# Moving stores between two DMA queues, and a prefetch by one unit, in a routed-attention and ELU-MLP kernel

## The chip, the cores and the metric

The kernel runs on one core of a Trainium2 chip. The metric is the device time of one execution in microseconds, lower is better. Five engines work beside each other, each on its own list of instructions in order: TensorE (PE, with its weight loads PEld), VectorE (DVE), ScalarE (ACT), GpSimd (POOL) and SyncE (SP). In this kernel SP does nothing but ask for DMAs, and what it asks for waits in the order in which it was written.

## The reference

Attention over q, k, v of shape (4, 8, 768, 64) in float32, in which a query sees only the keys of its own cluster, and then a two-layer MLP over the 3072 rows of 512 that come out:

```
mask = q_assign[:, :, :, None] == k_assign[:, :, None, :]
scores = np.where(mask, scale * np.matmul(q, k.transpose(0, 1, 3, 2)), -1000000000.0)
attn = softmax(scores)
x = np.matmul(attn, v)                  # -> (3072, 512)
h = x @ w_in                            # w_in (512, 2048)
g = np.where(h > 0.0, h, np.exp(np.minimum(h, 0.0)) - 1.0)
out = g @ w_out                         # w_out (2048, 512)
```

## The kernel before, in words

**Attention** comes first, in 32 slots of one batch, half a sequence and two heads each. Beside its last slots GpSimd prepares sums of x and of w_in for what follows, and VectorE still turns the last pieces of w_out, which arrive as 64-bit words, into float32 (`begin`, `join`, L306 to L350: L316 and L324, then ACT's L326, then L336, L340, L346). A piece's buffer comes free after L340, and then SP asks for the next (L296).

**The MLP** then takes six groups of 512 rows (k_ = 0 to 5). Each group has a first product (x times w_in, with the ELU) and a second (g times w_out). Both are done with a block scheme that needs seven block products in place of eight, at the price of sums and differences of blocks of weights and of activations.

*First product.* Four units u = 0 to 3 (`unit`, L752). A unit has seven block products of eight matmuls (L726), in this order: a11, s1, s2, a12, s3, s4, a22. a11, a12, s1 and a22 are parts of w_in itself; s2, s3 and s4 are sums of them, and stand in three places of the tile `spare` (`w_tmp`), which every unit uses again. In group 0 GpSimd computes them for the next unit (`w_step`, L705, L707, L709, one each for s2, s3, s4) and a DMA stores each in DRAM (`w_far`, L710). In groups 1 to 5 a DMA loads them back (L702). `w_step(k_, u + 1, n)` is called inside unit u: n = 0 and 1 in its body, n = 2 in `rest_of`, which runs at the start of the next unit (`flush_all`). Behind the products ACT copies banks (L766, L770, L775, L783) and takes the exponentials (L736), GpSimd clamps them (L737), VectorE adds banks (L776, L785) and finishes the ELU (L740, L802). The block s3 waits for ACT's copy L775, the block s4 for VectorE's L776.

*Second product.* Group 0 does it plainly (`second_product_plain`). Groups 1 to 5 do it once more by the block scheme (`second_product`, L1035, small products of four matmuls, L901). Its right sides are sums of parts of w_out, the tables. They are made once, in group 1, by `table_steps` (L850): seven parts of w_out, s3, s4, s2, a11, a12, s1, a22 in this order, four steps of VectorE each (L859, L862, L866, L869), with a store to DRAM after each (`far_w`; seven stores for s3, s4 and s2, three for the other four, called DIRECT). Results stand alternately in `sums_w` (`s_all`) and `p_out`. A unit of group 1 calls `fill_table`, two steps, four times, the last of them in `rest_of`.

*Streaming.* The second product reads the tables through ten places in SBUF (`slots_w`: four in `words_w`, five in `sums_w`, one in `p_out`). `fetch` (L896) loads the next in the order of use; after each use one more is fetched. The first ten are fetched after unit 2 of group 1 (L1174).

So on SP's list of group 1 stand, in the order of the code, the loads of `w_far`, the stores of the tables and the first ten fetches, and each of them waits for what stands ahead of it.

Of the kernel before, what the change touches and what calls it, by code (L numbers as in the profile page):

```python
# [61 lines left out]
def main_path(ctx, tc, c, q, k, v, centroids, moe_w_in, moe_w_out, out):  # L62


    nc = tc.nc
# [82 lines left out]
    slots_w = [words_w[:, ts(n, 512)] for n in range(4)]  # L148
# [525 lines left out]
    def x_parts(k_):  # L674
        a, b_ = slice(GS * k_, GS * k_ + QS), slice(GS * k_ + QS, GS * (k_ + 1))
        return X[:, :2, a], X[:, :2, b_], X[:, 2:, a], X[:, 2:, b_]
# [13 lines left out]
    def w_parts(u):  # L690
        low, high = slice(QS * u, QS * u + QS), slice(DF // 2 + QS * u, DF // 2 + QS * u + QS)
        return w_in[:, :2, low], w_in[:, 2:, low], w_in[:, :2, high], w_in[:, 2:, high]

    w_far = [[far.tile([P, 512], F32, name=f"w_far{u}{n}") for n in range(3)] for u in range(4)]

    def w_step(k_, u, n):

        a11, a12, s1, a22 = w_parts(u)
        s2, s3, s4 = (w_tmp[:, m] for m in range(3))
        flat = spare[:, 0, ts(n, 512)]  # L700
        if k_ > 0:
            nc.sync.dma_start(flat, w_far[u][n])  # L702
            return
        if n == 0:
            nc.gpsimd.tensor_tensor(s2, s1, a11, op=Alu.subtract)  # L705
        elif n == 1:
            nc.gpsimd.tensor_tensor(s3, a22, s2, op=Alu.subtract)  # L707
        else:
            nc.gpsimd.tensor_tensor(s4, a12, s2, op=Alu.subtract)  # L709
        nc.sync.dma_start(w_far[u][n], flat)  # L710

    def blanks(s):

        for bank in sets[s][1:3]:
            nc.tensor.matmul(
                bank,
                lhsT=blank,
                rhs=blank[:, 0:1].to_broadcast([P, 512]),
                start=True,
                stop=True,  # L720
            )

    def block_product(bank, left, right, first):
        for f in range(2):
            for ch in range(2):
                nc.tensor.matmul(  # L726
                    bank[:, ts(f, QS)],
                    lhsT=left[:, ch, ts(f, P)],
                    rhs=right[:, ch],
                    start=first and f == 0 and ch == 0,  # L730
                    stop=ch == 1,
                    skip_group_check=True,
                )

    def elu_exp(to, bank):
        nc.scalar.activation(to, bank.rearrange("p (f n) -> p f n", f=2), Act.Exp)  # L736
        nc.gpsimd.tensor_scalar(to, to, 1.0, 0.0, op0=Alu.min, op1=Alu.max)  # L737

    def elu(to, bank):
        nc.vector.scalar_tensor_tensor(  # L740
            to, to, -1.0, bank.rearrange("p (f n) -> p f n", f=2), op0=Alu.add, op1=Alu.max
        )
# [3 lines left out]
    def flush_all():  # L746
        flush()
        for other in behind:
            other()
        behind.clear()  # L750

    def unit(k_, u, after_second=None, fill=None):  # L752

        fill = fill or (lambda: None)
        x11, t3, x21, x22 = x_parts(k_)
        t1, t2, t4 = x_s
        a11, a12, s1, a22 = w_parts(u)
        s2, s3, s4 = (w_tmp[:, m] for m in range(3))
        b1, b2, b3, b4 = sets[(k_ + u) % 2]
        m5, u3 = stage[:, 0], stage[:, 1]  # L760
        low, high = slice(2 * u, 2 * u + 2), slice(FC // 2 + 2 * u, FC // 2 + 2 * u + 2)
        c11, c12 = g[:, low, :QS], g[:, low, QS:]
        c21, c22 = g[:, high, :QS], g[:, high, QS:]

        block_product(b1, a11, x11, True)
        nc.scalar.copy(b2, b1)  # L766
        flush_all()
        yield
        block_product(b4, s1, t1, True)
        nc.scalar.copy(m5, b4)  # L770
        if after_second is not None:
            after_second()
        yield
        block_product(b2, s2, t2, False)
        nc.scalar.copy(b3, b2)  # L775
        nc.vector.tensor_tensor(b2, b2, m5, op=Alu.add)  # L776
        fill()
        if u < 3:
            w_step(k_, u + 1, 0)
        block_product(b1, a12, x21, False)  # L780
        elu_exp(c11, b1)
        block_product(b3, s3, t3, False)
        nc.scalar.copy(u3, b3)  # L783
        elu(c11, b1)
        nc.vector.tensor_tensor(b4, b4, u3, op=Alu.add)  # L785
        if k_ > 0:
            for t in {2: ("t1",), 3: ("t2", "t3", "t4")}.get(u, ()):
                t_step(0, t)
        fill()
        block_product(b2, s4, x22, False)  # L790
        if u < 3:
            w_step(k_, u + 1, 1)
        elu_exp(c12, b2)
        elu_exp(c22, b4)
        fill()
        block_product(b3, a22, t4, False)

        def rest_of():
            elu_exp(c21, b3)
            elu(c12, b2)  # L800
            elu(c22, b4)
            nc.vector.tensor_tensor(c12, c22, c12, op=Alu.subtract)  # L802
            fill()
            elu(c21, b3)
            if u < 3:
                w_step(k_, u + 1, 2)

        behind.append(rest_of)
# [17 lines left out]
    DIRECT = ("a11", "a12", "s1", "a22")  # L826
# [3 lines left out]
    def part_w(a, i, j):  # L830
        return quad_w[a][:, 4 * j : 4 * j + 4, ts(i, P)]
# [15 lines left out]
    def flat_far(a, x):  # L847
        return far_w[a, x].rearrange("p (f m) -> p f m", m=P)

    def table_steps():  # L850

        for n, a in enumerate(("s3", "s4", "s2", "a11", "a12", "s1", "a22")):
            at = p_out[:, :1536] if n % 2 else s_all
            s3, s2, s4 = (at[:, ts(m, 512)].rearrange("p (f m) -> p f m", m=P) for m in range(3))
            q11, q12, q21, q22 = (part_w(a, i, j) for i in range(2) for j in range(2))
            if a not in DIRECT:
                for x, q_ in (("q11", q11), ("q12", q12), ("q22", q22)):
                    nc.sync.dma_start(flat_far(a, x), q_)
            nc.vector.tensor_tensor(s3, q11, q21, op=Alu.subtract)  # L859
            nc.sync.dma_start(flat_far(a, "s3"), s3)  # L860
            yield
            nc.vector.tensor_tensor(q21, q21, q22, op=Alu.add)  # L862
            if a not in DIRECT:
                nc.sync.dma_start(flat_far(a, "s1"), q21)
            yield
            nc.vector.tensor_tensor(s2, q21, q11, op=Alu.subtract)  # L866
            nc.sync.dma_start(flat_far(a, "s2"), s2)
            yield
            nc.vector.tensor_tensor(s4, q12, s2, op=Alu.subtract)  # L869
            nc.sync.dma_start(flat_far(a, "s4"), s4)  # L870
            yield

    WHICH = {"m1": "q11", "m2": "q12", "m3": "s4", "m4": "q22", "m5": "s1", "m6": "s2", "m7": "s3"}
    HERE = {"m1": (0, 0), "m2": (0, 1), "m4": (1, 1), "m5": (1, 0)}
# [18 lines left out]
    def fetch():  # L893
        nonlocal fetched
        if fetched < len(streamed):
            nc.sync.dma_start(slots_w[fetched % len(slots_w)], far_w[streamed[fetched]])  # L896
            fetched += 1
# [39 lines left out]
    def t_step(n, t):  # L937
        if n >= len(UNITS):
            return
        b = UNITS[n][2]  # L940
        q11, q12, q21, q22 = (part_g(b, i, j) for i in range(2) for j in range(2))
        to = t_of[t]
        if t == "t1":
            nc.vector.tensor_tensor(to, q12, q11, op=Alu.subtract)
        elif t == "t2":
            nc.vector.tensor_tensor(to, q22, t_of["t1"], op=Alu.subtract)
        elif t == "t3":
            nc.vector.tensor_tensor(to, q22, q12, op=Alu.subtract)
        else:
            nc.vector.tensor_tensor(to, q21, t_of["t2"], op=Alu.subtract)  # L950
# [191 lines left out]
    def run(steps_of):  # L1142
        for _ in steps_of:
            pass
# [7 lines left out]
    for u in range(4):  # L1152
        if u == 1:
            blanks(1)
        run(unit(0, u, finish_attention if u == 0 else None))
        weigh(len(blocks) + u)
        if u == 1:
            findings()
# [9 lines left out]
    for k_ in range(1, N // GS):  # L1168
        for u in range(4):
            if k_ == 1 and u < 2:  # L1170
                blanks((k_ + u) % 2)
            fill = fill_table if k_ == 1 else None
            run(ahead if ahead is not None and u == 0 else unit(k_, u, fill=fill))
            if k_ == 1 and u == 2:  # L1174
                for _ in slots_w:
                    fetch()
        ahead = unit(k_ + 1, 0) if k_ + 1 < N // GS else iter(())
        second_product(k_, ahead)

# [261 lines left out]
```

## Time and profile before

| what | value |
|---|---|
| median of 3 runs | 929.04 us (927.85 to 930.41) |
| the profiled execution | 928.16 us, its span from first to last instruction 926.4 us |
| granted TensorE clock, mean | 0.993 |
| PE busy | 901.5 us (97% of the span) |
| DVE, ACT, POOL busy | 672.4, 411.8, 200.8 us |
| DMA | 121.22 MB, 43.4% of the 16 engines' time on SP's queue, 0.6% on GpSimd's |

Times in the profile are in microseconds from the span's first instruction. Attention ends at about 344; group 0 has its first product from 344.6 to 397.8, group 1 from 448.5 to 507.3. A line of the timeline gives start, duration, engine, line of code, operation, what it writes and reads, how often, and in brackets how long the engine stood idle before it and who ended that. A line of the waits gives who waited for whom, total, number of times, and the longest.

### The profile page before, as it was taken

What the parts mean: (1) busy time and instruction counts of PE and PEld (TensorE: products, weight loads), DVE (VectorE), ACT (ScalarE), POOL (GpSimd) and SP (SyncE); (2) the same over time, 40 slices, a digit from 0 to 9 for tenths busy, and PEclk for the clock granted to TensorE, in tenths of its full rate; (3) what the DMA queues carried; (4) which work ended last, traced back from release to release, by engine and by line L of the source; (5) the groups of instructions that cost most, each with busy time, mean ns of one, the idle gap of its engine ahead of it and who ended that gap; (6) DMA issues with size and microseconds to landing.
All of it is one profiled execution on the core that took longest, in us unless ns stands there. A gap on an engine that the chain in (4) does not pass through costs nothing.

```text
span 926.4 us, 15836 instructions
## 1 busy us (share of the span) xinstructions
PE 901.5 (97%) x6080; PEld 686.9 (74%) x6083; DVE 672.4 (73%) x980; ACT 411.8 (44%) x811; POOL 200.8 (22%) x189
## 2 busy tenths in 40 slices
PE   7999999999999998999997999999999999999997
PEld 5444444444444457899986998899889988998997
DVE  5899999999999995952485953595459545953574
ACT  3777787777768663310132213321332133223321
POOL 1102021231314444730121202220222022202200
PEclk9999999999999999999997999999999999999999
DMA  6774565353425122110486762176317621762172
GB/s 174 213 187 105 136 135 103 108 114 78 111 98 162 58 83 80 65 38 2 154 264 219 231 202 91 35 234 199 91 35 244 204 77 35 251 205 69 38 221 88
DMA packets 144099, 121.22 MB, mean 131 GB/s; under 512 B 88208, under 2 KB 104592, under 8 KB 142992
## 3 DMA queue, kind: packets, MB, share of 16 engines
q1 hardware_dynamic: 143728, 119.08, 43.4%
q0 software_dynamic: 288, 1.05, 0.6%
q8 instruction: 50, 0.82, 0.4%
q14 instruction: 33, 0.27, 0.1%
HBM read 100.96 MB, written 18.09 MB: 129 GB/s over the span
## 4 chain that ended last, share of the span: by engine, by line
PE 80%; DVE 12%; DMA 3%; issue 1%; ACT 1%; SPq 1%; DVEq 0%; POOL 0%; ACTq 0%; POOLq 0%
PE bank L901 23%; PE bank L726 21%; PE banks L494 9%; PE o_bank L532 9%; PE o_bank L901 4%; PE o_bank L726 4%; PE d_bank L901 2%; PE banks L507 2%; PE d_bank L550 2%; PE d_bank L726 2%; DVE sums_w L524 2%; DVE sums_w L519 2%; DMA spare<-w_far 1%; DVE sums_w L525 1%; PE d_bank L423 1%
## 5 line engine op out<-in xcount | busy, mean ns | idle before, releaser
L516 ACT ACTIVATE p_out<-banks 128x768 f32<-128x768 f32 x192 | 154.3, 811 | 25.0 <-PE banks L507 23.5
L737 POOL TENSOR_SCALAR kq_g<-kq_g 128x512 f32<-128x512 f32 x96 | 71.3, 752 | 410.9 <-ACT kq_g L736 408.7
L532 PE MATMUL o_bank<-p_out,kq_g 128*64 128x384 f32 x768 | 129.3, 486 | 0.0
L532 PEld LDWEIGHTS o_bank<-p_out,kq_g 128*64 128x64 f32 x768 | 55.1, 137 | 68.8 <-issue 63.6
L740 DVE SCALAR_TENSOR_TENSOR kq_g<-kq_g,bank 128x512 f32<-128x512 f32 x72 | 48.3, 684 | 78.0 <-POOL kq_g L737 78.0
L726 PE MATMUL bank<-xT,w_in 128*128 128x256 f32 x384 | 90.7, 379 | 0.1
L568 POOL TENSOR_TENSOR xT<-xT,sums_w 128x384 f32<-128x384 f32 x32 | 35.9, 1120 | 206.5 <-DVE sums_w L565 161.7
L726 PEld LDWEIGHTS bank<-xT,w_in 128*128 128x128 f32 x384 | 72.6, 190 | 10.1
L726 PE MATMUL bank<-xT,spare 128*128 128x256 f32 x288 | 68.4, 387 | 8.9 <-DMA spare<-w_far 6.4
L726 PE MATMUL bank<-x_sum,w_in 128*128 128x256 f32 x288 | 69.3, 384 | 0.0
L726 PEld LDWEIGHTS bank<-xT,spare 128*128 128x128 f32 x288 | 55.6, 194 | 17.7 <-issue 7.2
L524 DVE TENSOR_TENSOR sums_w<-sums_w,p_out 128x1536 f32<-128x1536 f32 x32 | 61.4, 1918 | 3.3
L736 ACT ACTIVATE kq_g<-bank 128x512 f32<-128x512 f32 x72 | 41.8, 598 | 47.8 <-PE bank L726 47.8
L901 PE MATMUL bank<-w_out,kq_g 128*128 128x128 f32 x512 | 62.9, 275 | 0.0
L726 PEld LDWEIGHTS bank<-x_sum,w_in 128*128 128x128 f32 x288 | 55.6, 194 | 7.8
L901 PEld LDWEIGHTS bank<-w_out,kq_g 128*128 128x128 f32 x512 | 60.4, 192 | 0.3
L519 DVE TENSOR_TENSOR sums_w<-p_out 128x1536 f32<-128x1536 f32 x32 | 59.0, 1842 | 2.0 <-ACT p_out L516 2.0
L961 DVE TENSOR_TENSOR kq_g<-kq_g 128x1024 f32<-128x1024 f32 x36 | 43.8, 1223 | 5.3 <-PE bank L901 5.3
L459 POOL TENSOR_SCALAR kq_g<-w_out,big,minus 128x768 bf16<-128x768 bf16 x16 | 33.1, 2076 | 58.1 <-ACT w_out L452 55.1
L494 PE MATMUL banks<-kq_g 64*128 64x384 f32 x192 | 39.7, 492 | 0.8 <-ACT p_out L516 0.8
L494 PE MATMUL banks<-x_sum,xT 64*128 64x384 f32 x192 | 39.6, 493 | 0.6 <-ACT p_out L516 0.6
L494 PE MATMUL banks<-kq_g,xT 64*128 64x384 f32 x192 | 39.6, 491 | 0.0
(232 smaller groups left out, 1698.6 us busy)
## 6 DMA issues: line engine op xcount, KB each, us to landing
spare<-w_far SPq DMA_DIRECT2D x60, 256.0 KB, 2.7
kq_g<-in_v_dram SPq DMA_DIRECT2D x32, 384.0 KB, 3.8
sums_w<-far_s_s SPq DMA_DIRECT2D x40, 256.0 KB, 4.0
words_w<-far_s_s SPq DMA_DIRECT2D x29, 256.0 KB, 3.6
words_w<-in_moe_w_out_dram SPq DMA_DIRECT2D x6, 1024.0 KB, 4.9
out_dram<-p_out SPq DMA_DIRECT2D x24, 256.0 KB, 2.5
w_out<-in_q_dram SPq DMA_DIRECT2D x112, 48.0 KB, 2.5
words_w<-far_a_s SPq DMA_DIRECT2D x21, 256.0 KB, 3.5
```

The source lines that it names most:

```text
L494: nc.tensor.matmul(s[:, e, :HS], lhsT=kT[b % 2][pr][rows, ts(kt, P)], rhs=qT[half][pr][rows], start=True, stop=False,)
L516: nc.scalar.activation(probs[kt], s[:, :, :HS], Act.Exp, scale=SCALE)
L519: nc.vector.tensor_tensor(add_to, probs_all[:, : 4 * HS], probs_all[:, 4 * HS : 8 * HS], op=Alu.add)
L524: nc.vector.tensor_tensor(add_to, add_to, probs_all[:, 8 * HS :], op=Alu.add)
L532: nc.tensor.matmul(o_bank[64 * e : 64 * e + 64, :HS], lhsT=v_raw[n % 2][:, e, kt], rhs=probs[kt][:, e], start=(kt == 0), stop=(kt == NT - 1),)
L568: nc.gpsimd.tensor_tensor(x_of(n), x_of(n), r_of, op=Alu.mult)
L726: nc.tensor.matmul(bank[:, ts(f, QS)], lhsT=left[:, ch, ts(f, P)], rhs=right[:, ch], start=first and f == 0 and ch == 0, stop=ch == 1, ski ...
L736: nc.scalar.activation(to, bank.rearrange("p (f n) -> p f n", f=2), Act.Exp)
L737: nc.gpsimd.tensor_scalar(to, to, 1.0, 0.0, op0=Alu.min, op1=Alu.max)
L740: nc.vector.scalar_tensor_tensor(to, to, -1.0, bank.rearrange("p (f n) -> p f n", f=2), op0=Alu.add, op1=Alu.max)
L901: nc.tensor.matmul(bank[:, :P], lhsT=left[:, f], rhs=right[:, f], start=first and f == 0, stop=last and f == 3, skip_group_check=True,)
L961: nc.vector.tensor_tensor(b[to][:, f], b[x][:, f], b[y][:, f], op=op)
```

## The change

Three things. The stores of w_in's sums (12 in all) are asked for by GpSimd, not by SP. The stores of a table's parts are collected and issued after the second step of the next part, the last ones after all steps; nothing is stored before its sums exist, and nothing else in the steps changes. The first ten fetches are issued inside unit 3 of group 1, after its second block product, instead of after unit 2.

```diff
@@ w_step
-        nc.sync.dma_start(w_far[u][n], flat)
+        nc.gpsimd.dma_start(w_far[u][n], flat)
@@ unit, after the second block product
         if after_second is not None:
             after_second()
+        if k_ == 1 and u == 3:
+            for _ in slots_w:
+                fetch()
         yield
@@ table_steps
+        made = []
+
+        def keep_far():
+            for to, src in made:
+                nc.sync.dma_start(to, src)
+            made.clear()
+
         for n, a in enumerate(("s3", "s4", "s2", "a11", "a12", "s1", "a22")):
...
-            if a not in DIRECT:
-                for x, q_ in (("q11", q11), ("q12", q12), ("q22", q22)):
-                    nc.sync.dma_start(flat_far(a, x), q_)
             nc.vector.tensor_tensor(s3, q11, q21, op=Alu.subtract)
-            nc.sync.dma_start(flat_far(a, "s3"), s3)
             yield
             nc.vector.tensor_tensor(q21, q21, q22, op=Alu.add)
-            if a not in DIRECT:
-                nc.sync.dma_start(flat_far(a, "s1"), q21)
+            keep_far()
             yield
             nc.vector.tensor_tensor(s2, q21, q11, op=Alu.subtract)
-            nc.sync.dma_start(flat_far(a, "s2"), s2)
             yield
             nc.vector.tensor_tensor(s4, q12, s2, op=Alu.subtract)
-            nc.sync.dma_start(flat_far(a, "s4"), s4)
+            parts = [("s3", s3), ("s2", s2), ("s4", s4)]
+            if a not in DIRECT:
+                parts += [("q11", q11), ("q12", q12), ("q22", q22), ("s1", q21)]
+            made += [(flat_far(a, x), y) for x, y in parts]
             yield
+        keep_far()
@@ main loop
             run(ahead if ahead is not None and u == 0 else unit(k_, u, fill=fill))
-            if k_ == 1 and u == 2:
-                for _ in slots_w:
-                    fetch()
```

## The prediction, made before the changed kernel ran

> **What bounds the kernel now.** I read the page first: PE is busy 97% of the span, so a change of queues can only pay where PE stands still. So next the waits of PE alone between 340 and 510 us, where all that is edited runs:
>
> ```profile
> PE bank L726 <- DMA spare<-w_far: 6.4, 2, 6.1
> PE bank L726 <- ACT bank L775: 2.5, 1, 2.5
> PE o_bank L726 <- DVE o_bank L776: 0.4, 1, 0.4
> ```
>
> Three waits in 170 us. The first is for a load of w_in's sums (L702) in group 1, the other two lie in group 0. PE's timeline gives the place of the first (8 matmuls are one block product):
>
> ```profile
> 490.91 1.89 PE L726 MATMUL bank<-xT,w_in 128*128 128x256 f32 x8
> 492.64 1.89 PE L726 MATMUL bank<-xT,spare 128*128 128x256 f32 x8
> 500.68 3.75 PE L726 MATMUL bank<-xT,spare 128*128 128x256 f32 x8 [6.15 <-DMA spare<-w_far]
> 504.22 3.20 PE L726 MATMUL bank<-x_sum,w_in 128*128 128x256 f32 x8
> 507.26 1.05 PE L901 MATMUL bank<-w_out,kq_g 128*128 128x128 f32 x8
> ```
>
> Blocks start 1.73 apart (490.91 to 492.64). Unit 3's block s4 should start at 492.64 + 1.73 = 494.37 and starts at 500.68: 6.31 lost. It and the next then take 3.54 and 3.04, 3.12 more than twice 1.73. The windows view shows why: the granted clock is 0.63 between 494 and 508, 1.00 from 448 to 494. So the wait costs 9.4. The chain of waits names its cause:
>
> ```profile
> 489.44 5.31 DMA sums_w<-far_s_q
> 494.75 0.02 issue
> 494.77 0.02 SPq L702
> 494.78 0.03 issue
> 494.81 5.72 DMA spare<-w_far
> 500.54 0.14 issue
> 500.68 6.75 PE bank L726 x16
> ```
>
> The load of s4 stood on SP's list behind the ten fetches (487.47 to 492.75) and two stores. It was issued at 494.81, as the eighth issue before it landed, and then took 5.72, against a median of 2.7 for such loads. A smaller case, unit 1's s4, started at 470.12 for 469.69: 0.4.
>
> **Later fetches and tables: the gain.** In the new order unit 3 starts with `rest_of`, whose load of s4 then stands ahead of the fetches. It needs only that PE has read the s4 of unit 2 (block from 482.28, over by 484.2) and that the stores of a12 ahead of it are issued: VectorE's last sum for them (L869) starts at 486.08, SP's store was issued at once. So the load goes out near 486.5; even at the worst landing of that stretch, 5.8, it is there at 492.3, before 494.37. All of 9.4 goes, and the cold clock with it.
>
> What is late next? (a) Loads behind bursts of seven stores. I take 0.65 us of SP per store and a landing every 0.65 to 1.0, as the trace's single landings follow each other between 464 and 478. Burst s3 starts when its sums exist, 457.8 to 463.4; the load of unit 1's s4 behind it lands near 467.1, needed 469.69. Burst s4: load of unit 2's s2 near 472.7, needed 476.8. Burst s2: load of unit 2's s4 near 479.7, needed 481.9. Margins 2.6, 4.1, 2.2: cost nothing, and the 0.4 above goes too. (b) The fetches, on SP from 487 to 493 as now, no longer have PE standing still behind them: the second product starts at 497.5 instead of 507.26. Its first fetched part is read two blocks (1.8) later, 499.3; the first fetch landed at 491.8, and the last needs to be there far later. (c) VectorE's writes into `s_all` and `p_out`: a buffer is written again two parts later, its store having landed some 6 us before. Only a22's is close: the s3 store lands behind the fetches at about 501.3, and ACT's first copy into that place (L971) is due at 501.3. ACT may be late; PE next needs ACT for the block m4, four blocks (3.6) later. Nothing, unless the store is 3.6 late. (d) VectorE finishes c21 near 501.6 and t1 at 502.3, PE wants t1 at 502.9. Nothing, 0.5 in hand. Sum of this part: 9.4 + 0.4 = 9.8.
>
> **Stores by GpSimd: the cost.** On SP such an issue takes 0.32. What it frees there is nothing: SP waited 70 us for GpSimd between 300 and 392, but its next piece (L296) went out at 358.72, 0.02 after L340 freed the buffer; v's loads landed long before use; and the loads for group 1, behind the last store at 392.36, are needed only after 450. On GpSimd twelve issues are new. The only row of an issue there:
>
> ```profile
> L1118 POOL DMA_DIRECT2D w_in<-w_in x2: 1007/1079/1151, 286.2 to 287.0; - x2
> ```
>
> That is d = 1.08 by its length, but from the first start (286.21) to the next instruction of GpSimd (287.55) is 1.34 for two, d = 0.67. I take 0.86, between them. The first three lie beside attention, where GpSimd idles 2 us or more. The others stand ahead of the clamps L737:
>
> ```profile
> 352.81 1.29 POOL L705 TENSOR_TENSOR spare<-w_in 128x512 f32<-128x512 f32 x1
> 354.08 0.61 POOL L737 TENSOR_SCALAR kq_g<-kq_g 128x512 f32<-128x512 f32 x1
> 367.31 1.29 POOL L709 TENSOR_TENSOR spare<-w_in,spare 128x512 f32<-128x512 f32 x1
> 368.68 1.27 POOL L705 TENSOR_TENSOR spare<-w_in 128x512 f32<-128x512 f32 x1
> 369.92 0.61 POOL L737 TENSOR_SCALAR kq_g<-kq_g 128x512 f32<-128x512 f32 x1
> ```
>
> *Unit 0:* one issue after L705. VectorE stands idle 2.40 for that clamp (L740), and L785, L336, L340, the load of the last piece, L316, L324, ACT's L326 and L775 hang on it without a gap; at the end PE waits its 2.5. It waits d longer.
>
> *Unit 1:* two more issues ahead of the c11 clamp, so VectorE's run from L740 on is 3d late. It ends in L776 (379.54 to 380.24), which PE needs at 381.61, in hand 1.37 less 0.14 of latency. PE is d late itself, so it loses 2d - 1.23: 0.1 at 0.67, 0.9 at 1.08.
>
> *Unit 2:* two more ahead of its c11 clamp, and the s3 store of unit 1. GpSimd has idle 1.06, 0.52 and 0.58 there to take them up. Carried through, L740 comes at 382.5 to 383.0 (d = 0.67) or 384.6 to 385.1 (1.08) for 381.41, and the sums L371 to L375, which follow, are 1.0 or 3.1 late. VectorE has no gap from there to L776 of unit 3, for which PE already waits 0.4; so PE is late by 1.0 or 3.1 in all, the earlier losses being contained in it. Unit 3 issues none. Cost 2.0 at d = 0.86, ends 1.0 and 3.1. Less than zero is excluded: nothing that PE waits for stood behind those stores.
>
> [...] But the clamps L737 take up to 2.64 for 0.61 beside L371 to L375, so contention is real here. [...]
>
> [...]
>
> **The sum.** The profiled execution took 928.16. Less 9.8, plus 2.0: 920.4. The median of the runs lies 0.9 above it, so 921.3.
>
> **Rivals.**
> - *The wait moves* (0.12): the bursts hold the loads up. If a store took twice what I use, each burst would last 5 us longer, and with margins of 2.2 to 4.1 the three loads would be late by about 2.5, 1 and 3; with the a22 store late by a few us as well the sum loses 6 to 9. Then 927 to 930, no change. For it: 33 stores in fewer, denser runs, and landings that reach 4 us. Against: SP issues the same stores in the same 50 us, the DMA share is 0.76 there.
> [...]
> - *Cold clock or slow issues, gain whole* (0.12): cost 4 to 6, 923 to 926.
> - *It doesn't reorder SP* (0.02): if the load of s4 waited for something else than the list, only the 2.0 is left, 931; the chain above speaks against it.
>
> **How the numbers follow.** My forecast has 0.63: 918.8 to 923.9, costs of 1.0 to 3.1 and 1.5 for a run's scatter. With the third rival, the range is 918.3 to 927. A measurement here tells 0.3%, 2.8 us, from no change. Faster: 0.63 + 0.12 + a little of the first rival, 0.77; slower 0.11 + 0.02; same 0.10.
>
> **What would show it.** In the changed profile: PE has no wait for `spare<-w_far` above 1 us in group 1, the clock is about 1.00 from 494 to 508, first product of group 1 takes 49 us instead of 58.7. Twelve `w_far<-spare` rows on POOL, 0.7 to 1.1 each; PE's wait for L775 in unit 1 is 3.2 to 3.6 and waits for L776 appear in units 2 and 3; group 0's first product takes 1 to 3 longer. I am wrong if POOL's rows run to 2 us and more, or if PE waits for loads in units 1 and 2, or ACT L971 holds up the second product.

## The result, and the profile after

The changed kernel takes 923.29 us in the median of four runs (922.52 to 924.02), against 928.97 before: a ratio of 0.9938, 95% interval 0.9920 to 0.9955, 5.7 us less. Faster was forecast, with 921.3 as the likeliest time and 918.3 to 927.0 as the range. The profiled execution took 922.52, its span 920.7.

First PE, as the prediction read it. Its waits from 340 to 510 us:

```profile
PE bank L726 <- ACT bank L778: 3.6, 1, 3.6
PE bank L910 <- DVE p_out L953: 0.6, 1, 0.6
PE o_bank L726 <- DVE o_bank L779: 0.4, 1, 0.4
```

(Lines of code behind L770 have moved: L775 is now L778, L776 is L779, L896 is L905, L901 is L910, L944 is L953, and the table stores stand at L860.) The wait for `spare<-w_far` is gone, the wait in group 0 has grown by 1.1, and there is a new one of 0.6. PE's timeline where it waits in group 0, and in unit 3 of group 1:

```profile
369.37 3.52 PE L726 MATMUL bank<-xT,spare 128*128 128x256 f32 x8 [3.58 <-ACT bank L778]
372.73 1.89 PE L726 MATMUL o_bank<-xT,spare 128*128 128x256 f32 x8
...
493.61 1.89 PE L726 MATMUL bank<-xT,w_in 128*128 128x256 f32 x8
495.33 3.62 PE L726 MATMUL bank<-xT,spare 128*128 128x256 f32 x16
498.79 1.89 PE L726 MATMUL bank<-x_sum,w_in 128*128 128x256 f32 x8
500.51 1.05 PE L910 MATMUL bank<-w_out,kq_g 128*128 128x128 f32 x8
```

In unit 3 the blocks s3 and s4 follow each other so closely that they are one row of 16. The windows view from 494 to 508, first before and then after (the last three columns are the granted clock, the DMA share and GB/s):

```profile
494.00:508.00 14.00, 7.85 (x26) 6.17 (x25) 6.45 (x10) 1.67 (x3) 1.49 (x3) 0.63 0.51 190
```

```profile
494.00:508.00 14.00, 13.45 (x91) 12.46 (x91) 13.18 (x19) 4.98 (x13) 7.90 (x8) 1.00 0.79 281
```

On SP's timeline the load of s4 (L702) now stands ahead of the fetches (L905):

```profile
487.76 1.33 SPq L860 DMA_DIRECT2D far_a_s<-sums_w  x2
489.19 0.38 SPq L702 DMA_DIRECT2D spare<-w_far  x1
489.62 1.87 SPq L905 DMA_DIRECT2D words_w<-far_a_s  x4
```

And the row of the twelve stores that GpSimd asks for:

```profile
L710 POOL DMA_DIRECT2D w_far<-spare x12: 562/576/976, 313.6 to 395.8; - x12
its engine sat idle before it (us, times) until:
  POOL spare L705: 1.2, 4
  POOL spare L707: 1.2, 4
  POOL spare L709: 1.2, 4
```

An issue takes 0.576 in the median, and GpSimd waits 0.3 ahead of each (1.2 for four) for its own sum to be done. Where the time of the two profiled executions went, by the first matmul of each stage (each number is rounded for itself):

| stretch | before | after | difference |
|---|---|---|---|
| up to group 0 | 344.6 | 345.2 | +0.6 |
| first product of group 0 | 53.1 | 55.8 | +2.6 |
| second product of group 0 | 50.8 | 50.8 | 0 |
| first product of group 1 | 58.7 | 48.8 | -9.9 |
| second product of group 1 to the end | 419.1 | 420.2 | +1.0 |
| span | 926.4 | 920.7 | -5.7 |

The first row is not the change: the 0.6 is there by 15 us, ahead of all that was edited.

### The profile page after: what moved, and what is told of

Same layout as the page of the kernel before. It is cut to its first block, busy times and chain, and to the rows that moved or that the text cites. A ratio compares the mean times of both kernels' runs of the same rounds, so it can differ in the third digit from the quotient of the medians.

```text
span 920.7 us, 15833 instructions
## 1 busy us (share of the span) xinstructions
PE 900.6 (98%) x6080; PEld 686.5 (75%) x6083; DVE 672.9 (73%) x980; ACT 412.1 (45%) x811; POOL 207.4 (23%) x201
## 4 chain that ended last, share of the span: by engine, by line
PE 77%; DVE 15%; issue 3%; POOL 2%; ACT 1%; SPq 1%; DMA 1%; DVEq 0%; POOLq 0%; ACTq 0%
PE bank L910 22%; PE bank L726 21%; PE o_bank L532 8%; PE banks L494 8%; PE o_bank L910 4%; PE o_bank L726 4%; PE d_bank L910 2%; DVE sums_w L524 2%; DVE sums_w L519 2%; PE banks L507 2%; PE d_bank L726 2%; PE d_bank L550 2%; DVE sums_w L525 1%; POOL kq_g L737 1%; PE banks L573 1%
## 5 line engine op out<-in xcount | busy, mean ns | idle before, releaser
L726 PEld LDWEIGHTS bank<-xT,spare 128*128 128x128 f32 x288 | 55.7, 194 | 11.7 <-POOL kq_g L737 4.0
L910 PE MATMUL bank<-w_out,kq_g 128*128 128x128 f32 x512 | 62.9, 275 | 0.0
L910 PEld LDWEIGHTS bank<-w_out,kq_g 128*128 128x128 f32 x512 | 60.4, 192 | 0.3
```

Source lines behind the costliest of these rows:

```text
L726: nc.tensor.matmul(bank[:, ts(f, QS)], lhsT=left[:, ch, ts(f, P)], rhs=right[:, ch], start=first and f == 0 and ch == 0, stop=ch == 1, ski ...
L910: nc.tensor.matmul(bank[:, :P], lhsT=left[:, f], rhs=right[:, f], start=first and f == 0, stop=last and f == 3, skip_group_check=True,)
```

## The experiments

Each time has its own runs of the kernel before beside it on the same chip (medians 929.87 for the four kernels below the change, 929.70 for the next three, 928.79 for the last four), so ratios are compared. "Group 0" and "group 1" are lengths of their first products in the profiled execution.

| kernel | median us | ratio to before, 95% | group 0 | group 1 |
|---|---|---|---|---|
| the change | 923.29 | 0.9938 (0.9920 to 0.9955) | 55.8 | 48.8 |
| GpSimd's stores alone | 931.73 | 1.0024 (1.0014 to 1.0034) | 55.7 | 58.7 |
| the rest alone, stores on SP | 920.53 | 0.9903 (0.9889 to 0.9917) | 54.8 | 48.8 |
| later fetches alone | 921.24 | 0.9913 (0.9898 to 0.9929) | 54.8 | 49.7 |
| later table stores alone | 924.20 | 0.9952 (0.9933 to 0.9971) | 53.2 | 52.2 |
| change, 24 issues by GpSimd | 926.42 | 0.9971 (0.9959 to 0.9982) | 61.5 | 48.8 |
| change, zeros in group 0's wait | 922.46 | 0.9931 (0.9912 to 0.9951) | 55.6 | 48.8 |
| rest alone, clamp first | 922.51 | 0.9932 (0.9914 to 0.9950) | 56.1 | 48.8 |
| rest alone, zeros | 919.70 | 0.9906 (0.9891 to 0.9922) | 53.3 | 48.8 |
| before, zeros in group 1's wait | 927.15 | 0.9979 (0.9967 to 0.9990) | 53.2 | 56.3 |
| rest alone, tables earlier | 925.00 | 0.9959 (0.9944 to 0.9974) | 53.3 | 55.0 |
| rest alone, zeros, tables earlier | 923.79 | 0.9948 (0.9934 to 0.9962) | 53.0 | 55.2 |

**Taking the change apart.** My theory: group 0's loss is GpSimd's issues in series ahead of the clamps, and group 1's gain is the place of s4's load on SP's list. Rivals: the loss is TensorE's slow clock; the gain comes from collecting the stores, or from an SP that no longer waits for GpSimd.

```diff
-        nc.sync.dma_start(w_far[u][n], flat)
+        nc.gpsimd.dma_start(w_far[u][n], flat)     # this alone
```

> The kernel before, with the stores of w_in's sums asked for by GpSimd and nothing else changed. Issue theory (each store delays the clamps behind it on GpSimd): group 0's first product 53.1 to about 55.8, group 1's stays 58.7, time 929.0 + 2.6 = 931.6, 2 more where the slow clock lasts longer. Rival (freeing SP is worth something, as GpSimd's waits on its list suggest): 929 or less.

It is slower by 0.24% or 2.2 us, and group 0 by 2.5; PE's wait for L775 is 3.4. An SP free of those stores was worth nothing.

```diff
-        nc.gpsimd.dma_start(w_far[u][n], flat)
+        nc.sync.dma_start(w_far[u][n], flat)       # in the changed kernel
```

> The changed kernel with the stores of w_in's sums back on SP. Issue theory: group 0 back to 53.1, group 1 at 48.8, so 923.3 - 2.6 = 920.7 or a little less. Rival (the change needs SP free of those stores): 923 or more.

0.9903: the change is 0.35% better without its first third. That profile's group 0 is 54.8 and not 53.1, though nothing was edited there. The wait in it is the same 2.5, but the granted clock went down behind it, 0.88 in the mean from 362 to 376 for 1.00 before; more on that below.

```diff
+        if k_ == 1 and u == 3:          # the kernel before, fetches moved, no more
+            for _ in slots_w:
+                fetch()
```

> The kernel before with the first ten fetches inside unit 3, table stores and w_in's stores as before. Fetch theory (the gain is that unit 3's load of s4 stands ahead of the fetches): 929.0 - 9.4 + 0.8 for the wait for t1 = 920.4, with the 0.3 wait for unit 1's s4 still there. Rival (the gain comes from collecting the table stores): 927 or more, with a wait of several us for spare<-w_far in unit 3.

As forecast: 9.1 of group 1's 9.9 come from this edit alone. Of the wait for the loads two short ones of 0.2 are left (PE's waits from 340 to 520):

```profile
PE bank L904 <- DVE p_out L947: 0.6, 1, 0.6
PE bank L726 <- DMA spare<-w_far: 0.4, 2, 0.2
```

What collecting the stores adds to it is 0.9 in group 1, which the times can't tell apart (0.9913 and 0.9903).

The last of the four collects the stores and leaves the fetches after unit 2:

> The kernel before with the table stores collected and a part later, fetches and w_in's stores as before. Fetch theory: the 6 us wait in unit 3 stays, unit 1's 0.3 goes, time 928.5 to 929. Rival (collecting the stores is the gain): near 920.

My expectation failed: 924.2, not 928.5 to 929. SP's timeline in this kernel (fetches are L902, stores L857):

```profile
486.08 1.83 SPq L902 DMA_DIRECT2D words_w<-far_a_s  x4
...
490.37 0.60 SPq L902 DMA_DIRECT2D p_out<-far_s_q  x1
491.07 0.61 SPq L702 DMA_DIRECT2D spare<-w_far  x1
492.44 1.60 SPq L857 DMA_DIRECT2D far_s_s<-p_out  x3
494.39 0.32 SPq L857 DMA_DIRECT2D far_a_s<-sums_w  x1
```

The load still stands behind ten fetches, but the three stores of s1 (L857 at 492.44), one of which stood ahead of the fetches and two between them and the load, now stand behind it. So it goes out at 491.07 instead of 494.81 and lands at 497.21; PE waits 3.2 instead of 6.2, and the clock stayed up in this profile: the block behind the wait takes 1.80, where it took 3.54 before. Group 1 is 6.5 shorter in it, but it is the fastest of six executions; the median, 2.4 above it, is 0.48% below the kernel before. The two edits are two cures of one wait: the later fetches take nearly all of it away and the later stores about half, which is why their gains don't add. "Collecting is no help" was wrong, and "collecting is the gain" is wrong too: moving the fetches alone does as much as both.

**Is group 0's loss the issues or the clock?** In the changed kernel's profile both are there: PE waits 3.58 for L778, and the clock is at half from 369.1 to 372.5, so that the block from 369.37 lasts until 372.73, 3.36 instead of 1.73. First, twice as many issues:

```diff
-        nc.gpsimd.dma_start(w_far[u][n], flat)
+        for m in range(2):
+            nc.gpsimd.dma_start(w_far[u][n][:, ts(m, 256)], flat[:, ts(m, 256)])
```

> The changed kernel with each of the twelve stores split in two, so 24 issues by GpSimd. Issue theory: a second issue costs its 0.58 without a new wait of 0.3; about five of them lie in series ahead of the clamps, at 5.5 us of path per us of issue about 3 more: 926.3. Rival (the slow clock of TensorE is the loss, the issues are hidden): within 1 of the changed kernel, 922.5 to 924.5.

926.42 for a forecast of 926.3: 0.9971 against 0.9938, 0.33% or 3.1 us. In its profile a pair of issues takes 1.13. (That one execution took 928.23 at a mean clock of 0.992, for 0.995 in the median of the eleven, so its 61.5 is more than the median lost.) Then zeros, to keep the clock up:

```diff
         block_product(b1, a12, x21, False)
+        if k_ == 0 and u == 1:
+            for _ in range(12):
+                nc.tensor.matmul(b1, lhsT=blank, rhs=blank[:, 0:1].to_broadcast([P, 512]), start=False, stop=True, ...)
```

> The changed kernel with twelve matmuls by zeros (they add nothing to the bank, 2.6 us of work) in the place where TensorE waits in unit 1 of group 0. Slow-clock theory: the clock stays at 1.00 there, group 0's first product falls from 55.8 by 1.6 or more, time 921.5 or less, and the runs scatter less. Issue theory: the clock stays up but TensorE then waits longer for L779 in units 2 and 3, so at most 0.9 is won, 922.4 to 923.3.

PE's waits from 340 to 510 in this kernel (its L920 and L963 are L910 and L953 of the changed one):

```profile
PE o_bank L726 <- DVE o_bank L779: 1.4, 1, 1.4
PE bank L726 <- ACT bank L778: 1.0, 1, 1.0
PE bank L920 <- DVE p_out L963: 0.6, 1, 0.6
PE bank L726 <- DVE bank L779: 0.2, 1, 0.2
```

The clock stayed up (0.999 in the mean of this execution, 0.997 in the changed kernel's), and group 0 is as long as before: 55.6 for 55.8. PE only waits elsewhere, for VectorE's L779 in unit 2 (0.2) and unit 3 (1.4 for 0.4). That is the chain by GpSimd and VectorE, which sets the end of group 0 with the clock or without it: VectorE's L779 in unit 3 starts at 396.54 here and at 396.60 in the changed kernel. Nor did the zeros delay this chain: GpSimd's first clamp behind them starts at 368.38, for 368.34. The median fell by 0.8, which the intervals can't tell from nothing.

**What can be won on top.** Without GpSimd's issues the chain is short again, and then the slow clock should cost:

```diff
+            for _ in range(9):          # stores on SP, in the same place
...                                      # the same matmul by zeros
```

> The changed kernel with w_in's stores back on SP, and nine matmuls by zeros (1.9 us, they add nothing) where TensorE waits in unit 1 of group 0. With that wait at 2.5 us the slow clock came in the profile of the version without zeros and made group 0 1.6 longer (54.8 for 53.1). Slow-clock theory: group 0 at 53.1 or less, median 1 to 1.6 below 920.5, 919 to 919.6, less scatter. Rival (VectorE's chain sets group 0, as it did with GpSimd's stores): no difference, 920 to 921.

The windows view from 362 to 376, first without the zeros and then with them (the third column from the right is the granted clock):

```profile
362.00:376.00 14.00, 11.52 (x46) 9.55 (x45) 9.18 (x12) 4.79 (x8) 6.87 (x7) 0.88 0.25 97
```

```profile
362.00:376.00 14.00, 13.26 (x62) 10.54 (x61) 9.20 (x12) 5.19 (x9) 7.86 (x7) 1.00 0.26 102
```

In the profiles group 0 falls from 54.8 to 53.3. The five runs lie within 0.6 (919.59 to 920.15), the six without the zeros, on another chip, within 2.3 (919.22 to 921.47). The ratios, 0.9906 and 0.9903, are the same: perhaps a steadier time, not one shown to be shorter. Either beats the changed kernel and the one before.

The same trick in the kernel before splits the old wait into its two parts:

```diff
+        if k_ == 1 and u == 3:
...                                      # 24 matmuls by zeros into b2, 5.4 us
         block_product(b2, s4, x22, False)
```

> The kernel before with 24 matmuls by zeros (5.2 us, they add nothing) ahead of block s4 of unit 3 in group 1, where TensorE waits 6.2 us for its load. If 6.3 of the 9.4 lost there is the wait and 3.1 the slow clock after it: the clock stays at 1.00, group 1 falls from 58.7 to 55.6 and the time by 3, to about 926.5. If the clock's record overstates it: less than 1.

```profile
495.79 5.39 PE L792 MATMUL bank<-blank 128*128 128x512 bf16 x24
501.93 1.99 PE L726 MATMUL bank<-xT,spare 128*128 128x256 f32 x8 [0.75 <-DMA spare<-w_far]
503.76 1.89 PE L726 MATMUL bank<-x_sum,w_in 128*128 128x256 f32 x8
```

s4 still starts 6.1 late (501.93 for 494.06 + 1.73 = 495.79), but it and a22 now take their normal 1.8 and 1.7, together 3.56 for 6.58 before: 3.0 were the slow clock. Group 1 is only 2.4 shorter, because unit 1's s4 waited 1.0 in this profile for 0.3 before; the time falls by 0.21% or 2.0 us. So of the 9.4 that I put down to this wait, 3 are the slow clock behind it, and the rest is the wait itself. Why the medians show 2.0 and not more, no run tells for certain; the longer wait in unit 1 would be 0.7 of it.

Two ideas failed. The first puts GpSimd's clamp of c11 ahead of its sum for s2, to shorten the chain further:

```diff
-        if u < 3:
+        if u < 3 and k_ > 0:
             w_step(k_, u + 1, 0)
         block_product(b1, a12, x21, False)
         elu_exp(c11, b1)
+        if u < 3 and k_ == 0:
+            w_step(k_, u + 1, 0)
```

> The changed kernel with w_in's stores on SP and, in group 0, GpSimd's clamp of c11 ahead of its sum for the next unit's s2 (1.3 us). Issue theory carried on (what stands ahead of the clamp on GpSimd sets group 0): the wait in unit 1 falls from 2.5 to about 1.2, time 1 to 2 below the one without this, 919 to 920. Rival (the load of the last piece or VectorE sets it anyway): no difference.

It is slower: 0.9932 for 0.9903. VectorE's timeline of this kernel says how (L790 and L788 here are the changed kernel's bank sum L788 and ACT's copy L786):

```profile
355.62 0.70 DVE L790 TENSOR_TENSOR bank<-bank,spare 128x512 f32<-128x512 f32 x1 [0.38 <-ACT spare L788]
356.23 1.98 DVE L336 SCALAR_TENSOR_TENSOR sums_w<-words_w,sums_w 128x1024 uint32<-128x1024 uint32 x1
...
385.78 3.07 DVE L371 TENSOR_TENSOR w_out<-w_out 128x2048 f32<-128x2048 f32 x1
```

The early clamp is capped at once, since VectorE's next bank sum waits for ACT (0.38). And L336 takes 1.98 for 1.22, and L371 3.07 for 2.28, in the kernel without this edit: they now run beside GpSimd's sum L707 and its clamps, whose start has moved. PE's wait in unit 1 is 3.0 instead of 2.5, its wait for L779 in unit 3 1.2 instead of 0.4.

The second makes the tables earlier, to spare VectorE the last steps where the new wait of 0.6 (for t1) stands:

```diff
     def fill_table():
-        next(table, None)
-        next(table, None)
+        for _ in range(3 if filled < 4 else 2):
+            next(table, None)
```

> The changed kernel with w_in's stores on SP, and three table steps instead of two in the first four calls, so that all 28 are over before unit 3's second call and VectorE has 2 to 3 us less to do at the start of the second product. Theory (the table's last steps there make t1 late): the 0.6 wait for t1 goes, 0.6 to 0.9 below 920.5. [...]

PE's waits from 446 to 510 in it, all of them, and the load that PE waits for, on SP's timeline:

```profile
PE bank L726 <- DVE p_out L874: 2.9, 1, 2.9
```

```profile
463.76 1.80 SPq L860 DMA_DIRECT2D far_s_s<-p_out  x3
465.91 2.11 SPq L860 DMA_DIRECT2D far_s_q<-sums_w  x3
468.06 0.91 SPq L860 DMA_DIRECT2D far_s_s<-sums_w  x1
469.07 0.91 SPq L702 DMA_DIRECT2D spare<-w_far  x1
```

The wait for t1 is gone, so without the table's last steps (1.09 and 0.69 us of VectorE in the changed kernel) t1 comes in time. But two bursts of seven stores now lie close together ahead of unit 1's s4; its load goes out at 469.07 and lands at 472.87, and PE starts that block at 473.00. (The view names the DVE instruction that ended in the same moment.) 2.9 of waiting and a slow clock behind it, with two blocks of 3.55 and 3.03 for 1.73 each, make group 1 55.0 for 48.8, and the time 0.9959.

> The last two together: 920.5 less the sum of what each won, 918.3 to 919 if both theories hold.

The zeros in group 0 and the earlier tables together make 0.9948, no better for the same reason: PE waits 3.3 for `spare<-w_far` there.

## Why the prediction was right, and where it was off

The direction and both mechanisms held. The profiled span should have fallen by 9.8 - 2.0 = 7.8 and fell by 5.7; the 2.1 that are missing are the 0.6 at the start, 0.6 in group 0, 1.0 behind the second product's start, less 0.1 in group 1.

*Later fetches and tables, 9.8.* Group 1 gave 9.9. The load of s4 went out at 489.19, which is 486.5 of the old count (this stretch runs 2.7 later), where the prediction put it, and landed at 492.25, 4.8 ahead of its use (495.33 + 1.73 = 497.06). One reading on the way was wrong without harm: VectorE's L869 starts at 485.07 and is over at 486.05; 486.08 is SP's store behind it. The clock from 494 to 508 is 1.00 for 0.63. The split within this term, "6.31 lost" and 3.12 for the clock, is confirmed by the zeros, with 3.0 for the second.

*(a), "Margins 2.6, 4.1, 2.2: cost nothing".* They cost nothing, but the margins were 1.8, 2.2 and 0.3: the loads landed at 471.09, 477.63 and 484.71 for blocks due at 472.89, 479.79 and 484.97. I took 0.65 per store on SP; single ones took up to 1.35, and the lag adds up over three bursts. The rival that the wait moves missed by 0.3 us, so that this term cost nothing was in part luck, and the kernel with the earlier tables is that rival. From 500 to the end PE has no wait but the one of the next point, so (b) and (c) cost nothing.

*(d), "Nothing, 0.5 in hand".* This step failed. PE waited 0.55 for t1 (L953), and the last matmuls come 0.8 later after the second product's start than before. VectorE at that place:

```profile
499.74 1.09 DVE L959 TENSOR_TENSOR p_out<-kq_g,p_out 128x512 f32<-128x512 f32 x1
500.76 1.09 DVE L872 TENSOR_TENSOR sums_w<-w_out 128x512 f32<-128x512 f32 x1
...
503.81 1.04 DVE L805 TENSOR_TENSOR kq_g<-kq_g 128x512 f32<-128x512 f32 x1
504.77 0.68 DVE L740 SCALAR_TENSOR_TENSOR kq_g<-kq_g,bank 128x512 f32<-128x512 f32 x1
505.37 1.16 DVE L953 TENSOR_TENSOR p_out<-kq_g 128x512 f32<-128x512 f32 x1
```

Four of them take 1.04 to 1.16, where I had used 0.69 throughout: 1.6 us more than reckoned, against 0.5 in hand. GpSimd's clamps and sums ran beside them (POOL is busy 7.9 of the 14 us from 494 to 508, before 1.5). Before, one of the four had been as long, beside GpSimd's L682, and I had not read it; the other three had run with GpSimd idle. Two of these three and the long one in the profile before:

```profile
497.04 0.68 DVE L950 TENSOR_TENSOR p_out<-kq_g,p_out 128x512 f32<-128x512 f32 x1
507.11 0.69 DVE L802 TENSOR_TENSOR kq_g<-kq_g 128x512 f32<-128x512 f32 x1
510.44 1.15 DVE L944 TENSOR_TENSOR p_out<-kq_g 128x512 f32<-128x512 f32 x1
```

(L950, L802 and L944 of before are L959, L805 and L953.) For those three the old wait of 6 us had kept the two engines apart; without it their work falls together. In the kernel with only the fetches moved the same 0.6 stands. The stretched sums were not enough by themselves: without the table's last steps there was no wait, though L959 and L953 were still as long. That unstretched sums would have left none either is only reckoned (1.6 against a wait of 0.55); no run shows it.

*Stores by GpSimd, 2.0.* Measured 2.6 in the profile and 2.2 alone in the medians. I took d = 0.86 between two readings of L1118. It is 0.576 and 0.30 of waiting, 0.88 together: the shorter reading of the row, 0.67, was the nearer for the issue, and the wait for GpSimd's own sum, which no row showed, made up the rest. So 0.86 came out by luck, and the "0.7 to 1.1" of the rows did not. "5.5 us of path per us of issue" gave 3.1 for the doubled issues, and 3.1 came; but it was an estimate, 2.1 / 0.38, and the prediction's two ends (1.0 at 0.67, 3.1 at 1.08) give 2.1 / 0.41 = 5.1, with which it is 2.9.

*"Waits for L776 appear in units 2 and 3".* In the changed kernel they didn't: none in unit 2 and 0.4, as before, in unit 3. The slow clock had already made PE late by the same amount. With the zeros, and the clock up, they appear, 0.2 and 1.4: the two hide each other.

*"Slower 0.11 + 0.02".* The 0.11 stood for issues of GpSimd that are much longer beside VectorE, and no run shows such issues: the one at 386.64 took 0.58 and landed after 2.33 while VectorE ran L371 (386.29 to 388.57), like the one at 383.75 with VectorE idle (0.56 and 2.32), and the longest of the twelve took 0.98. The cost would have eaten the gain only near 1.08 + 6.7 / 5.1 = 2.4 for each, an estimate from the two ends above (6.7 is 9.8 less 3.1).

*"Cold clock or slow issues", 4 to 6.* No run with twelve stores shows such a cost: the stores alone cost 2.2, and they and the slow clock together 2.6 in group 0. The clock was at half for 3.4 us behind the wait of 3.58 in the changed kernel, and for 10.2 behind the one of 6.15 in the kernel before. Behind shorter waits the runs show both. It came down behind 2.5 in the rest alone (0.88 from 362 to 376) and behind 2.9 with the earlier tables (blocks of 3.55 and 3.03 for 1.73). It stayed up behind 2.5 in the kernel before (1.00 from 362 to 376) and behind 3.2 with the later table stores alone (a block of 1.80). The measurement decides: such a wait can cost the clock, and which one does the runs don't tell.

## What to carry to other kernels

A load that PE needs soon and a prefetch that it needs much later should not stand on one in-order queue with the prefetch ahead (6.15 us of PE's time here); find what stands ahead of the late load before deciding to move the queue. That a queue waits long for an engine says nothing of a gain (SP's 70 us here, and 1.0024 without them): ask what behind it was late. And reckon an issue on a compute engine at its own length plus the wait for what it stores (0.576 and 0.30 on GpSimd here), times the number that lie in series ahead of something that PE waits for.

## What the runs showed of the hardware that I had not expected

In both traces, of the kernel before and of the changed one, an issue by SP went out only after the eighth issue before it had landed: 494.81 for one that landed at 494.75. The six issues from 491.84 to 495.45 of the kernel before each follow that landing by 0.01 to 0.07, and of its 511 issues and the 499 of the changed kernel none goes out ahead of it. Whether the program or the chip sets the eight, no run here shows. So not only what stood ahead of the load counted, but how long the last eight took.

With the clamp first, VectorE's L371 took 3.07 for 2.28 and L336 1.98 for 1.22 beside GpSimd's moved sum and clamps, a third to two thirds more, so that this reordering on GpSimd alone cost more than it won (0.9932 for 0.9903).

And behind waits of 2.5 to 3.6 us TensorE's clock was at half in some profiles (3.4 us of it behind 3.58 in the changed kernel) and at 1.00 in others (behind 2.5 in the kernel before). Where nothing else hid it, in the rest alone, group 0 took 54.8 with it and 53.3 with the zeros.
